# The last loads of a decode kernel: K, K, V, gate and up ahead of the last V, and W_down last in 10 KB rows

## The chip, the cores and the metric

The kernel runs on one core of one Trainium2 chip. The metric is the device time of one execution in microseconds (us). All executions quoted here are of the fast state. Times are medians; a ratio is the mean time of one kernel's fast runs over that of the kernel before in the same rounds, so it is not quite the ratio of the medians quoted beside it. The span of a profile runs from the first to the last instruction and is about 2 us shorter than the time.

## The reference

One decode step of a pre-LayerNorm block, in bf16: B = 2 rows, D = 512, 32 heads of 128, a cache of 8,192 positions, F = 1,376.

```python
h   = x + softmax(q k^T / sqrt(128)) v @ wo       # q = layernorm(x) @ wq, k and v from the cache
u   = layernorm(h)
out = h + (relu(u @ W_gate) * (u @ W_up)) @ W_down
```

K and V caches are 268 MB; all weights together are 12.6 MB. One core reads all of it.

## The kernel before

The 64 (row, head) combinations are handled as 32 pairs, 0 to 31; K31 and V31 are the tiles of the last pair. A pair needs one K tile and one V tile, 4 MB each, as 128 partitions of 32 KB. Four slots hold the tiles: K in slots 0 and 2, V in slots 1 and 3. VectorE (DVE) computes three quarters of the scores by multiply and tree-add, TensorE (PE) the rest by transposes; ScalarE (ACT) takes the exponentials; PE does the PV matmuls with V as the loaded weights.

```python
for p in range(NP):                                   # NP = 32 pairs
    ...                                               # scores and exp of pair p
    if p + 2 < NP:
        sp.wait(*t_kfree[p])
        t_k[p + 2] = load(s, slot[s][:], kv(A_k_cache, p + 2))
    if p == NP - 2:
        sp.wait(*t_kfree[p])                          # slot 0 is free: the weights go there
        nc.sync.dma_start(slot[s][:, 0:DC * F], B_W_gate...)
        nc.sync.dma_start(slot[s][:, DC * F:2 * DC * F], B_W_up...)
        nc.sync.dma_start(slot[s][...].rearrange("p (r n) -> p r n", n=D),
                          B_W_down[0:1280].rearrange("(r p) n -> p r n", p=128))   # 1,280 rows of 1 KB
        nc.sync.dma_start(wd_last[0:FR, :], B_W_down[1280:F])                      # 96 rows of 1 KB
    ...                                               # PV matmuls of pair p
    if p + 2 < NP - 1:
        sp.wait(t_pv[p])
        t_v[p + 2] = load(sv, ...)                    # V one pair behind K
    if p == NP - 2:
        ...                                           # V31 in four pieces, behind the weights
    if p == 14:
        nc.sync.dma_start(wo_sb[:], ...)              # W_o, 4,096 rows of 1 KB
```

After the last PV the tail is a chain: 40 W_o matmuls, the residual, the mean, up and gate (44 matmuls each), a variance sum in float32, W_down (44), the output.

```python
lhsT=w[:, c, f * 128:f * 128 + fw]                    # up and gate: contiguous columns
...
nc.tensor.matmul(Sp[0][:, 64:64 + B], lhsT=ones_f[:], rhs=d2[:, c * B:(c + 1) * B], ...)  # float32, 4 of them
```

The softmax here doesn't subtract the row's maximum and nothing guards it: scores larger than these inputs give would overflow.

## Time and profile before

| | before |
|---|---|
| time (three runs; the result below has a fourth) | 682.75 us (682.70 to 682.88) |
| span | 680.7 us |
| V31 issued | 651.1 us |
| last piece of V31 landed, last PV ended | 667.8, 668.4 us |
| from the last PV's end to the end | 12.3 us |

From the timeline of the kernel before, the DMA issues of the sync engine at the end (start, duration, queue, line, operation, destination and source, count):

```profile
617.86 0.33 SPq L133 DMA_DIRECT2D slot<-in_A_k_cache_dram  x1
637.52 0.33 SPq L377 DMA_DIRECT2D slot<-in_B_W_gate_dram  x1
637.90 0.97 SPq L379 DMA_DIRECT2D slot<-in_B_W_up_dram  x1
638.92 0.52 SPq L381 DMA_DIRECT2D slot<-in_B_W_down_dram  x1
639.48 11.62 SPq L384 DMA_DIRECT2D wd_last<-in_B_W_down_dram  x1
651.14 2.02 SPq L426 DMA_DIRECT2D slot<-in_A_v_cache_dram  x4
```

The issue behind W_down's 1,280 rows takes 11.62 us, so V31 is issued only at 651.14. From the windows of one microsecond of the kernel before (stretch and length, busy us and instructions of PE, PE's weight loads, DVE, ACT and GpSimd, then granted PE clock, busy share of the DMA engines, GB/s):

```profile
650.00:651.00 1.00, 0.69 (x11) 0.34 (x9) 0.98 (x1) 0.96 (x2) 0.00 (x0) 0.50 0.48 203
651.00:652.00 1.00, 0.38 (x8) 0.29 (x8) 0.96 (x1) 0.53 (x2) 0.00 (x0) 0.50 0.49 183
652.00:653.00 1.00, 0.00 (x0) 0.00 (x0) 0.93 (x3) 0.66 (x4) 0.00 (x0) 0.50 0.72 219
```

For two microseconds about half of the DMA engine time stands idle there.

From the timeline of the kernel before, the tail (in brackets the idle time before and what ended it):

```profile
667.84 0.59 PE L407 MATMUL O<-e,slot 128*128 128x2 bf16 x16 [0.62 <-DMA slot<-in_A_v_cache_dram]
...
668.28 1.48 PE L303 MATMUL W<-O_sb,wo_sb 128*128 128x2 bf16 x40
...
670.95 1.52 PE L473 MATMUL S<-d_b,slot 128*128 128x2 bf16 x44 [0.66 <-DVE S L462]
...
672.33 1.52 PE L473 MATMUL O<-d_b,slot 128*128 128x2 bf16 x44
...
673.72 1.84 PE L482 MATMUL S<-d,ones_f 128*128 128x2 f32 x8
...
675.42 0.47 PE L501 MATMUL O<-hd,slot 128*128 128x2 bf16 x10
```

The W_down matmuls (675.42) stand behind the float32 variance sum in PE's order, although what they need was ready at 674.15. The weight loads of up and W_o in the kernel before, by line (duration in ns: least, median, most):

```profile
L303 PEld LDWEIGHTS W<-O_sb,wo_sb x136: 111/118/123, 585.4 to 669.6; 128*128 128x128 bf16 x136
```

```profile
L473 PEld LDWEIGHTS S<-d_b,slot x44: 103/104/195, 670.9 to 672.2; 128*128 128x128 bf16 x40, 128*96 128x96 bf16 x4
```

W_o is read in steps of 8 bytes (118 ns), up in contiguous columns (104 ns).

### The profile page before, as it was taken

The numbers are of one execution on the slowest core, as the hardware profiler recorded it, in microseconds if no ns is written. First come the engines' busy times: TensorE is split into PE (matmuls) and PEld (weight loads), VectorE is DVE, ScalarE is ACT, GpSimd is POOL, SyncE is SP. The second block draws the span as 40 slices with busy tenths as digits, with TensorE's granted clock in tenths as the row PEclk, the third lists the DMA queues.
The fourth block names the chain that finished last, engine by engine and source line by source line (L and its number), as shares of the span: only waits on it lengthen the run. The fifth ranks groups of instructions, "written<-read, shape, count | busy, mean of one in ns | idle before, by whom it ended". The sixth has DMA issues, their size and how long they took to land.

```text
span 680.7 us, 14440 instructions
## 1 busy us (share of the span) xinstructions
PE 297.6 (44%) x6602; PEld 268.7 (39%) x6602; DVE 492.9 (72%) x426; ACT 202.6 (30%) x523; POOL 1.8 (0%) x11
## 2 busy tenths in 40 slices
PE   2544334444543445354342344535443444653436
PEld 2444334443433334344341333434433443543326
DVE  1777778867777887777782788776777886777781
ACT  0632223333222333332131233333222333332230
POOL 1000000000000000000000000000000000000000
PEclk9955566555555555655555556555556555555555
DMA  9999999999999999999999999999999999999990
GB/s 374 437 432 431 428 428 430 430 429 430 432 429 431 430 429 429 430 430 429 430 345 435 429 428 428 428 430 431 428 429 430 429 429 430 430 429 430 409 360 27
DMA packets 15936, 281.97 MB, mean 414 GB/s; under 512 B 1442, under 2 KB 6916, under 8 KB 7172
## 3 DMA queue, kind: packets, MB, share of 16 engines
q1 hardware_dynamic: 15872, 281.06, 97.1%
q8 instruction: 51, 0.84, 0.5%
q14 instruction: 9, 0.07, 0.0%
q10 hardware_dynamic: 4, 0.00, 0.0%
HBM read 281.05 MB, written 0.00 MB: 413 GB/s over the span
## 4 chain that ended last, share of the span: by engine, by line
DMA 69%; DVE 27%; SPq 2%; PE 1%; issue 1%; DVEq 0%
DMA slot<-in_A_k_cache_dram 66%; DVE prod L324 16%; DVE tb L332 6%; DVE prod L332 3%; DMA slot<-in_A_v_cache_dram 2%; SPq L384 2%; DVE scores L339 1%; PE S L482 0%; PE S L473 0%; PE O L501 0%; PE O L473 0%; PE W L303 0%; SPq L426 0%; SPq L133 0%; SPq L379 0%
## 5 line engine op out<-in xcount | busy, mean ns | idle before, releaser
L324 DVE TENSOR_TENSOR prod<-slot,q_b 128x6144 bf16<-128x6144 bf16 x64 | 214.9, 3358 | 135.3 <-DMA slot<-in_A_k_cache_dram 134.2
L407 PE MATMUL O<-e,slot 128*128 128x2 bf16 x4096 | 119.5, 165 | 248.4 <-ACT e L261 124.2
L407 PEld LDWEIGHTS O<-e,slot 128*128 128x128 bf16 x4096 | 114.4, 104 | 253.6 <-DMA slot<-in_A_v_cache_dram 126.9
L355 ACT ACTIVATE kT<-T 128x1024 bf16<-128x1024 bf16 x128 | 126.9, 1022 | 171.7 <-PE T L349 170.7
L349 PE MATMUL T<-ident,slot 128*128 128x128 bf16 x1024 | 123.6, 307 | 71.9 <-DMA slot<-in_A_k_cache_dram 71.9
L332 DVE TENSOR_TENSOR tb<-prod 128x3072 bf16<-128x3072 bf16 (+1 forms) x128 | 148.2, 1158 | 4.4
L349 PEld LDWEIGHTS T<-ident,slot 128*128 128x128 bf16 x1024 | 100.3, 141 | 74.9 <-DMA slot<-in_A_k_cache_dram 74.9
L261 ACT ACTIVATE e<-scores 64x48 bf16<-64x48 f32 x128 | 32.8, 256 | 255.0 <-DVE scores L339 253.4
L332 DVE TENSOR_TENSOR prod<-tb 128x1536 bf16<-128x1536 bf16 (+1 forms) x128 | 84.2, 658 | 4.4
L253 PE MATMUL S<-qT,kT 128*128 128x2 bf16 x1024 | 48.4, 168 | 33.0 <-ACT kT L355 31.7
L253 PEld LDWEIGHTS S<-qT,kT 128*128 128x128 bf16 x1024 | 41.1, 107 | 52.0 <-ACT kT L355 52.0
L339 DVE TENSOR_REDUCE scores<-prod 128x48 f32<-128x384 bf16 x64 | 35.4, 553 | 2.2
L261 ACT ACTIVATION_READ_ACCUMULATOR e<-scores 64x1 f32 x128 | 23.7, 185 | 0.0
L261 ACT ACTIVATE e<-S 64x32 bf16<-64x32 f32 x64 | 13.0, 204 | 15.1 <-PE S L253 14.3
L261 ACT ACTIVATION_READ_ACCUMULATOR e<-S 64x1 f32 x64 | 12.9, 201 | 0.7
L235 ACT ACTIVATE q_b<-O 128x512 bf16<-128x512 f32 x8 | 4.3, 594 | 15.6 <-PE O L230 15.6
L208 DVE CAST qT<-W 128x64 bf16<-128x64 f32 x1 | 0.2, 225 | 12.0 <-PE W L203 12.0
L203 PE MATMUL W<-xlT,slot 128*128 128x2 bf16 x128 | 3.6, 165 | 8.6 <-DMA slot<-in_A_wq_dram 8.6
L203 PEld LDWEIGHTS W<-xlT,slot 128*128 128x128 bf16 x128 | 3.5, 104 | 8.7 <-DMA slot<-in_A_wq_dram 8.7
L279 DVE TENSOR_REDUCE zr<-O 128x16 f32<-128x48 f32 (+1 forms) x4 | 0.8, 204 | 8.3 <-PE O L271 8.3
L271 PE MATMUL S<-zs,ones_f 128*128 128x6 f32 x2 | 0.6, 367 | 10.9 <-ACT e L261 10.9
L230 PE MATMUL O<-ident,qrep 128*128 128x128 bf16 x32 | 4.3, 303 | 1.7 <-ACT q_b L235 0.9
(56 smaller groups left out, 47.2 us busy)
## 6 DMA issues: line engine op xcount, KB each, us to landing
slot<-in_A_k_cache_dram SPq DMA_DIRECT2D x32, 4096.0 KB, 27.9
slot<-in_A_v_cache_dram SPq DMA_DIRECT2D x31, 4096.0 KB, 32.1
slot<-in_A_wq_dram SPq DMA_DIRECT2D x1, 4096.0 KB, 12.3
wo_sb<-in_A_wo_dram SPq DMA_DIRECT2D x1, 4096.0 KB, 43.4
slot<-in_A_v_cache_dram SPq DMA_DIRECT2D x2, 1536.0 KB, 12.1
slot<-in_B_W_gate_dram SPq DMA_DIRECT2D x1, 1376.0 KB, 10.0
slot<-in_B_W_up_dram SPq DMA_DIRECT2D x1, 1376.0 KB, 13.2
slot<-in_B_W_down_dram SPq DMA_DIRECT2D x1, 1280.0 KB, 15.0
```

Source lines behind the costliest of these rows:

```text
L203: i = nc.tensor.matmul(Wp[:, h * B:(h + 1) * B], lhsT=wq[:, c, h * Dh:(h + 1) * Dh], rhs=lT[:, c * B:(c + 1) * B], start=(c == 0), stop=(c ...
L230: i = nc.tensor.matmul(Op[m % 2][:, k * 128:(k + 1) * 128], lhsT=qrep[m % 2][:, k * 128:(k + 1) * 128], rhs=ident[:], start=True, stop=True)
L235: t_cp[m] = act.run(nc.scalar.activation(out=q_b[:, m * 512:(m + 1) * 512], in_=Op[m % 2][:], func=ACT.Copy))
L253: i = nc.tensor.matmul(Sp[p % 2][:, 2 * jj:2 * jj + 2], lhsT=kT[n % 3][:, k * 128:(k + 1) * 128], rhs=qT[:, 2 * p:2 * p + 2], start=True, ...
L261: t = act.run(nc.scalar.activation(out=e_t[p % 2][q, j0:j0 + nj, a], in_=src(q, a), func=ACT.Exp, scale=inv_sqrt_dh, accum_out=zs[q, 2 * p ...
L324: t_dm = dve.run(nc.vector.tensor_tensor(out=prod[:], in0=k_t[:, c * JC:(c + 1) * JC, :], in1=qv, op=ALU.mult))
L332: dve.run(nc.vector.tensor_tensor(out=o, in0=cur[:, :, 0:half], in1=cur[:, :, half:w], op=ALU.add))
L339: t_s = dve.run(nc.vector.tensor_reduce(out=sc[:], in_=cur, axis=AX.X, op=ALU.add))
L349: i = nc.tensor.transpose(Tp[n % 3][:, k * 128:(k + 1) * 128], k_t[:, j, :], ident[:])
L355: t_ev[n] = act.run(nc.scalar.activation(out=kT[n % 3][:], in_=Tp[n % 3][:], func=ACT.Copy))
L384: nc.sync.dma_start(wd_last[0:FR, :], B_W_down[1280:F]).then_inc(sem_w, 16)
L407: i = nc.tensor.matmul(Op[k % 2][:, col:col + 2], lhsT=v_t[:, j, :], rhs=e_t[p % 2][:, j, :], start=(nmm == 0), stop=(nmm == J - 1))
```

## The change

The intent: bring W_down, which is needed last, behind the last V; make its rows long; bring K31 early, so that the scores of the last pair are done when V31 comes; and shorten the tail. W_o moves to the start, into the buffer that W_q leaves free. Rows of 10 KB put rows 10p to 10p+9 of W_down on partition p, so that the hidden units of block f are f, f+10, f+20, ...: the columns of gate and up must be read in steps of 10 elements, 20 bytes.

```diff
-                t_wq = load(3, slot[3][:], A_wq...)
+                nc.sync.dma_start(X[:], A_wq...).then_inc(sem_wq, 16)
@@ after the q projection
+                nc.sync.dma_start(X[:].rearrange("p (h n) -> p h n", n=D),
+                    A_wo.rearrange("(h d) n -> d h n", d=128)).then_inc(sem_wo, 16)
@@ the pair loop (cut)
+                vparts = ((0, 96, 128), (1, 0, 48), (2, 48, 88), (2, 88, 96))
+                    if p < NP - 2:
+                        pv(p)
+                        if p < NP - 4:
+                            load_v(p + 2)
+                        elif p == NP - 3:
+                            load_v(p + 1)          # V30, issued behind K31
+                    elif p == NP - 2:
+                        sp.wait(*t_kfree[p])
+                        for k, w in enumerate((B_W_up, B_W_gate)):
+                            nc.sync.dma_start(slot[0][:, k * DC * F:(k + 1) * DC * F], ...)
+                        load_v(p + 1, vparts)      # V31 in four pieces
+                        nc.sync.dma_start(slot[0][:, 2 * DC * F:2 * DC * F + 10 * D],
+                            B_W_down[0:10 * 128].rearrange("(p r) n -> p (r n)", r=10)).then_inc(sem_wd, 16)
@@ before the last PV
+                o_proj(range(HM, 30), 0, 2)        # HM = 24; this and the next line: 32 of the 40 W_o matmuls
+                o_proj(range(30, 32), 0, 1)
@@ up and gate
-                                dst[...], lhsT=w[:, c, f * 128:f * 128 + fw],
+                                dst[...], lhsT=w[:, c, f:1280:10] if f < 10 else w[:, c, 1280:F],
@@ variance
-                    i = nc.tensor.matmul(Sp[0][:, 64:64 + B], lhsT=ones_f[:], rhs=d2[...])      # x4, float32
+                    i = nc.tensor.matmul(Sp[0][:, 64:64 + B], lhsT=onesn[:], rhs=vh[...])       # x2, bf16
```

Also cut: the gate's result and W_down are split in halves, wd_last is loaded at the start, two memsets of PSUM go, W_down's matmuls loop over blocks first, the first 96 W_o matmuls run at pair 24 instead of 27, and some small tiles share memory with others.

More of the change, by code (lines that the diff above doesn't have):

```diff
@@ L87, in bass_sequential_preLN__gqa_block_cached__glu_gated_reglu__decode_kernel @@
         slot_cnt = [0] * 4
-        sem_x, sem_wo, sem_w, sem_wdl, sem_out = S("x"), S("wo"), S("w"), S("wdl"), S("out")
+        sem_x, sem_wq, sem_wo, sem_w, sem_wd, sem_out = S("x"), S("wq"), S("wo"), S("w"), S("wd"), S("out")
         sem_vl = [S(f"vl{i}") for i in range(4)]
         slot = [sb(f"slot{i}", [128, SLOT], BF16) for i in range(4)]
-        wo_sb = sb("wo_sb", [128, H, D], BF16)
-        wd_last = sb("wd_last", [128, D], BF16)
+        HM = 24
+        X = sb("X", [128, H * D], BF16)
+        wd_last = sb("wd_last", [FR, D], BF16)
         prod = sb("prod", [128, JC, Dh], BF16)
@@ L97, in bass_sequential_preLN__gqa_block_cached__glu_gated_reglu__decode_kernel @@
         q_b = sb("q_b", [128, NP * Dh], BF16)
-        qrep = [sb(f"qrep{i}", [128, 4 * 128], BF16) for i in range(2)]
         qT = sb("qT", [128, NP * 2], BF16)
@@ L103, in bass_sequential_preLN__gqa_block_cached__glu_gated_reglu__decode_kernel @@
         onesn = sb("onesn", [128, 128], BF16)
-        x_row = sb("x_row", [B, D], BF16)
-        lnx_row = sb("lnx_row", [B, D], BF16)
+        qrep = [tb[:, i * 512:(i + 1) * 512] for i in range(2)]
+        x_row = kT[0][0:B, 0:D]
+        lnx_row = kT[0][0:B, D:2 * D]
         bst = sb("bst", [B, 6], F32)
@@ L121, in bass_sequential_preLN__gqa_block_cached__glu_gated_reglu__decode_kernel @@
         r2 = sb("r2", [128, B], F32)
+        vh = sb("vh", [128, 2 * B], BF16)
         u_sb = sb("u_sb", [128, FC * B], F32)
@@ L146, in _ @@
             def _(eng):
-                nc.scalar.dma_start(x_row[:], A_x[:, 0]).then_inc(sem_x, 16)
-                t_wq = load(3, slot[3][:], A_wq.rearrange("(p c) n -> p (c n)", c=DC))
+                nc.scalar.dma_start(x_row, A_x[:, 0]).then_inc(sem_x, 16)
+                nc.sync.dma_start(X[:], A_wq.rearrange("(p c) n -> p (c n)", c=DC)).then_inc(sem_wq, 16)
                 t_k, t_v = {}, {}
@@ L153, in _ @@
                 t_k[1] = load(2, slot[2][:], kv(A_k_cache, 1))
+                t_v[1] = load(3, slot[3][:], kv(A_v_cache, 1))
+                nc.sync.dma_start(wd_last[:], B_W_down[F - FR:]).then_inc(sem_wd, 16)
                 pool.run(nc.gpsimd.memset(ident_f[:], 0.0))
@@ L170, in _ @@
                 dve.wait((sem_x, 16))
-                dve.run(nc.vector.bn_stats(out=bst[:], in_=x_row[:]))
+                dve.run(nc.vector.bn_stats(out=bst[:], in_=x_row))
                 dve.last()
@@ L181, in _ @@
                 t_ln = dve.run(nc.vector.tensor_scalar(
-                    out=lnx_row[:], in0=x_row[:], scalar1=mv[:, 0:1], scalar2=sd[:, 0:1],
+                    out=lnx_row, in0=x_row, scalar1=mv[:, 0:1], scalar2=sd[:, 0:1],
                     op0=ALU.subtract, op1=ALU.mult))
@@ L187, in _ @@
                 for k, row in enumerate((x_row, lnx_row)):
-                    rv = row[:].rearrange("b (n c) -> b c n", c=DC)
+                    rv = row.rearrange("b (n c) -> b c n", c=DC)
                     for c in range(DC):
@@ L196, in _ @@
                 lT = xlT[:, DC * B:]
-                wq = slot[3][:].rearrange("p (c n) -> p c n", c=DC)
-                pe.wait(t_wq, t_xlT)
+                wq = X[:].rearrange("p (c n) -> p c n", c=DC)
+                pe.wait((sem_wq, 16), t_xlT)
                 for h in range(H):
@@ L211, in _ @@
                 sp.wait(t_q)
-                t_v[1] = load(3, slot[3][:], kv(A_v_cache, 1))
+                nc.sync.dma_start(
+                    X[:].rearrange("p (h n) -> p h n", n=D),
+                    A_wo.rearrange("(h d) n -> d h n", d=128)).then_inc(sem_wo, 16)
                 t_cp = {}
@@ L221, in _ @@
                     t = dve.run(nc.vector.tensor_copy(
-                        out=qrep[m % 2][:].rearrange("p (k r) -> p k r", r=64),
+                        out=qrep[m % 2].rearrange("p (k r) -> p k r", r=64),
                         in_=qT[:, m * 8:(m + 1) * 8].unsqueeze(2).broadcast_to([128, 8, 64])))
@@ L293, in o_scale @@
                         op=ALU.mult))
-                wo_v = wo_sb[:].rearrange("p h (n c) -> p h c n", c=DC)
+                wo_m = X[:].rearrange("p (h n c) -> p h c n", n=128, c=DC)
                 Ov = O_sb[:].rearrange("p (g b a) -> p g a b", b=B, a=2)
@@ L303, in o_proj @@
                             i = nc.tensor.matmul(
-                                Wp[:, c * B + b0:c * B + b1], lhsT=wo_v[:, h, c, :], rhs=Ov[:, h // 2, h % 2, b0:b1],
+                                Wp[:, c * B + b0:c * B + b1], lhsT=wo_m[:, h, c, :], rhs=Ov[:, h // 2, h % 2, b0:b1],
                                 start=first[0], stop=last, skip_group_check=True)
@@ L311, in _, with pv, load_v @@
                 t_batch = {}
+                vparts = ((0, 96, 128), (1, 0, 48), (2, 48, 88), (2, 88, 96))
+                W_AT = 24
+                def pv(p):
+                    v_t = tile((2 * p + 1) % 4)
+                    k = next(kk for kk, (a, b_) in enumerate(batches) if a <= p < b_)
+                    col = 2 * (p - batches[k][0])
+                    parts = vparts if p == NP - 1 else (
+                        [(0, NCH * JC, J)] + [(1 + c, c * JC, (c + 1) * JC) for c in range(NCH)])
+                    if p == batches[k][0] and k >= 2:
+                        pe.wait(t_O[k - 2])
+                    nmm = 0
+                    for ci, (ei, j0, j1) in enumerate(parts):
+                        pe.wait(t_exp[p][ei], (sem_vl[ci], 16) if p == NP - 1 else t_v[p])
+                        for j in range(j0, j1):
+                            i = nc.tensor.matmul(
+                                Op[k % 2][:, col:col + 2], lhsT=v_t[:, j, :], rhs=e_t[p % 2][:, j, :],
+                                start=(nmm == 0), stop=(nmm == J - 1))
+                            nmm += 1
+                    t_pv[p] = pe.run(i)
+                    if p + 1 in ends and p < NP - 1:
+                        t_batch[k] = z_sum(k, *batches[k])
+                        if k < 3:
+                            t_O[k] = normalize(k, *batches[k], t_batch[k], False)
+                def load_v(p, parts=None):
+                    sv = (2 * p + 1) % 4
+                    if p >= 2:
+                        sp.wait(t_pv[p - 2])
+                    if parts is None:
+                        t_v[p] = load(sv, slot[sv][:], kv(A_v_cache, p))
+                        return
+                    src = kv(A_v_cache, p)
+                    for ci, (_, j0, j1) in enumerate(parts):
+                        nc.sync.dma_start(
+                            slot[sv][:, j0 * Dh:j1 * Dh], src[:, j0 * Dh:j1 * Dh]).then_inc(sem_vl[ci], 16)
                 for p in range(NP):
@@ L315, in _ @@
                     k_t = tile(s)
-                    last_pair = p == NP - 1
                     for c in range(NCH):
@@ L366, in _ @@
                         exp(p, 1 + c, lambda q, a: sc[q, :], c * JC, JC)
-                        if last_pair and c == 0:
-                            t_O[3] = normalize(3, 24, 31, t_batch[3], False)
                     t_kfree[p] = (t_dm, t_pt[p * NG + NG - 1])
@@ L374, in _ @@
                         t_k[p + 2] = load(s, slot[s][:], kv(A_k_cache, p + 2))
-                    if p == NP - 2:
-                        sp.wait(*t_kfree[p])
-                        nc.sync.dma_start(slot[s][:, 0:DC * F], B_W_gate.rearrange("(p c) n -> p (c n)", c=DC)
-                                          ).then_inc(sem_w, 16)
-                        nc.sync.dma_start(slot[s][:, DC * F:2 * DC * F],
-                                          B_W_up.rearrange("(p c) n -> p (c n)", c=DC)).then_inc(sem_w, 16)
-                        nc.sync.dma_start(
-                            slot[s][:, 2 * DC * F:2 * DC * F + 10 * D].rearrange("p (r n) -> p r n", n=D),
-                            B_W_down[0:1280].rearrange("(r p) n -> p r n", p=128)).then_inc(sem_w, 16)
-                        nc.sync.dma_start(wd_last[0:FR, :], B_W_down[1280:F]).then_inc(sem_w, 16)
-                        ws = s
@@ L388, in _ @@
-                    sv = (2 * p + 1) % 4
-                    v_t = tile(sv)
-                    k = next(kk for kk, (a, b_) in enumerate(batches) if a <= p < b_)
-                    col = 2 * (p - batches[k][0])
-                    if not last_pair:
-                        pe.wait(t_v[p])
-                        order = [(0, NCH * JC, J)] + [(1 + c, c * JC, (c + 1) * JC) for c in range(NCH)]
-                    else:
-                        order = [(1, 0, 48), (2, 48, 96), (0, 96, 112), (0, 112, 128)]
-                        zt = z_sum(4, 31, 32)
-                        normalize(4, 31, 32, zt, True)
@@ L399, in _ @@
-                    if p == batches[k][0] and k >= 2:
-                        pe.wait(t_O[k - 2])
-                    nmm = 0
-                    for ci, (ei, j0, j1) in enumerate(order):
-                        pe.wait(t_exp[p][ei])
-                        if last_pair:
-                            pe.wait((sem_vl[ci], 16))
-                        for j in range(j0, j1):
-                            i = nc.tensor.matmul(
-                                Op[k % 2][:, col:col + 2], lhsT=v_t[:, j, :], rhs=e_t[p % 2][:, j, :],
-                                start=(nmm == 0), stop=(nmm == J - 1))
-                            nmm += 1
@@ L411, in _ @@
-                    t_pv[p] = pe.run(i)
-                    if p + 1 in ends and not last_pair:
-                        t_batch[k] = z_sum(k, *batches[k])
-                        if k < 3:
-                            t_O[k] = normalize(k, *batches[k], t_batch[k], False)
-                    if p + 2 < NP - 1:
-                        sp.wait(t_pv[p])
-                        t_v[p + 2] = load(sv, slot[sv][:], kv(A_v_cache, p + 2))
-                    elif p + 2 == NP - 1:
-                        t_vlast = t_pv[p]
@@ L421, in _ @@
-                    if p == NP - 2:
-                        sp.wait(t_vlast)
-                        sl = (2 * (p + 1) + 1) % 4
-                        src = kv(A_v_cache, p + 1)
-                        for ci, (j0, j1) in enumerate(((0, 48), (48, 96), (96, 112), (112, 128))):
-                            nc.sync.dma_start(
-                                slot[sl][:, j0 * Dh:j1 * Dh], src[:, j0 * Dh:j1 * Dh]).then_inc(sem_vl[ci], 16)
-                    if p == 14:
-                        nc.sync.dma_start(wo_sb[:], A_wo.rearrange("(h d) n -> d h n", d=128)).then_inc(sem_wo, 16)
@@ L430, in _ @@
-                    if p == 27:
-                        pe.wait((sem_wo, 16), t_O[0], t_O[1], t_O[2])
-                        o_proj(range(0, 24), 0, 2)
-                    if p == NP - 2:
-                        pass
+                    if p < NP - 2:
+                        pv(p)
+                        if p == W_AT:
+                            pe.wait((sem_wo, 16), t_O[0], t_O[1], t_O[2])
+                            t_om = pe.run(o_proj(range(0, HM), 0, 2))
+                        if p < NP - 4:
[3 more added lines that the diff above has]
+                    elif p == NP - 2:
+                        sp.wait(*t_kfree[p])
+                        for k, w in enumerate((B_W_up, B_W_gate)):
+                            nc.sync.dma_start(
+                                slot[0][:, k * DC * F:(k + 1) * DC * F],
+                                w.rearrange("(p c) n -> p (c n)", c=DC)).then_inc(sem_w, 16)
+                        load_v(p + 1, vparts)
+                        nc.sync.dma_start(
+                            slot[0][:, 2 * DC * F:2 * DC * F + 10 * D],
+                            B_W_down[0:10 * 128].rearrange("(p r) n -> p (r n)", r=10)).then_inc(sem_wd, 16)
@@ L437, in _ @@
+                pv(NP - 2)
+                t_O[3] = normalize(3, 24, 31, t_batch[3], False)
                 pe.wait(t_O[3])
-                o_proj(range(24, 30), 0, 2)
+                o_proj(range(HM, 30), 0, 2)
                 o_proj(range(30, 32), 0, 1)
+                normalize(4, 31, 32, z_sum(4, 31, 32), True)
+                pv(NP - 1)
                 dve.wait(t_pv[NP - 1])
@@ L457, in _, with ffn_in @@
                     in1=Sp[0][:, 0:B].unsqueeze(1).broadcast_to([128, DC, B]), op=ALU.subtract))
-                dve.last()
-                t_d2 = dve.run(nc.vector.tensor_tensor(out=d2[:], in0=d_b[:], in1=d_b[:], op=ALU.mult))
-                dve.run(nc.vector.memset(Op[1][:, 0:FC * B], 0.0))
-                t_m0 = dve.run(nc.vector.memset(Sp[1][:, 0:FC * B], 0.0))
-                wgt = slot[ws][:, 0:DC * F].rearrange("p (c f) -> p c f", c=DC)
-                wup = slot[ws][:, DC * F:2 * DC * F].rearrange("p (c f) -> p c f", c=DC)
-                wdn = slot[ws][:, 2 * DC * F:2 * DC * F + 10 * D].rearrange("p (r n c) -> p r c n", c=DC, n=128)
+                wup, wgt = (slot[0][:, k * DC * F:(k + 1) * DC * F].rearrange("p (c f) -> p c f", c=DC)
+                            for k in range(2))
+                wdn = slot[0][:, 2 * DC * F:2 * DC * F + 10 * D].rearrange("p (r n c) -> p r c n", c=DC, n=128)
                 wdl = wd_last[:].rearrange("p (n c) -> p c n", c=DC)
-                pe.wait((sem_w, 64), t_d, t_m0)
-                def ffn_in(dst, w):
-                    for f in range(FC):
+                pe.wait((sem_w, 32), t_d)
+                def ffn_in(dst, w, f0, f1):
+                    for f in range(f0, f1):
                         fw = 128 if f < 10 else FR
@@ L473, in ffn_in @@
                             i = nc.tensor.matmul(
-                                dst[0:fw, f * B:(f + 1) * B], lhsT=w[:, c, f * 128:f * 128 + fw],
+                                dst[0:fw, f * B:(f + 1) * B], lhsT=w[:, c, f:1280:10] if f < 10 else w[:, c, 1280:F],
                                 rhs=d_b[:, c * B:(c + 1) * B], start=(c == 0), stop=(c == DC - 1))
                     return pe.run(i)
-                t_u = ffn_in(Sp[1], wup)
-                t_g = ffn_in(Op[1], wgt)
-                pe.wait(t_d2)
-                for c in range(DC):
-                    i = nc.tensor.matmul(Sp[0][:, 64:64 + B], lhsT=ones_f[:], rhs=d2[:, c * B:(c + 1) * B],
-                                         start=(c == 0), stop=(c == DC - 1))
-                t_var = pe.run(i)
+                FH = 6
+                t_u = ffn_in(Sp[1], wup, 0, FC)
+                t_g = (ffn_in(Op[1], wgt, 0, FH), ffn_in(Wp, wgt, FH, FC))
+                dve.last()
+                dve.run(nc.vector.tensor_tensor(out=d2[:], in0=d_b[:], in1=d_b[:], op=ALU.mult))
+                dve.last()
+                dve.run(nc.vector.tensor_reduce(
+                    out=vr[:], in_=d2[:].rearrange("p (c b) -> p b c", b=B), axis=AX.X, op=ALU.add))
+                dve.last()
+                dve.run(nc.vector.tensor_copy(out=vh[:, 0:B], in_=vr[:]))
+                dve.last()
+                t_vh = dve.run(nc.vector.tensor_tensor(out=vh[:, B:], in0=vr[:], in1=vh[:, 0:B], op=ALU.subtract))
                 dve.wait(t_u)
@@ L487, in _ @@
                 dve.last()
-                dve.wait(t_g)
-                t_hd = dve.run(nc.vector.scalar_tensor_tensor(
-                    out=hd[:], in0=Op[1][:, 0:FC * B], scalar=0.0, in1=u_sb[:], op0=ALU.max, op1=ALU.mult))
+                t_hd = []
+                for k, (bank, f0, f1) in enumerate(((Op[1], 0, FH), (Wp, FH, FC))):
+                    dve.wait(t_g[k])
+                    t_hd.append(dve.run(nc.vector.scalar_tensor_tensor(
+                        out=hd[:, f0 * B:f1 * B], in0=bank[:, f0 * B:f1 * B], scalar=0.0,
+                        in1=u_sb[:, f0 * B:f1 * B], op0=ALU.max, op1=ALU.mult)))
+                pe.wait(t_vh)
+                for k in range(2):
+                    i = nc.tensor.matmul(Sp[0][:, 64:64 + B], lhsT=onesn[:], rhs=vh[:, k * B:(k + 1) * B],
+                                         start=(k == 0), stop=(k == 1))
+                t_var = pe.run(i)
                 dve.wait(t_var)
-                dve.run(nc.vector.tensor_scalar(
-                    out=vr[:], in0=Sp[0][:, 64:64 + B], scalar1=1.0 / D, scalar2=eps, op0=ALU.mult, op1=ALU.add))
+                dve.run(nc.vector.tensor_scalar_add(out=vr[:], in0=Sp[0][:, 64:64 + B], scalar1=eps))
                 dve.last()
                 dve.run(nc.vector.reciprocal(out=r2[:], in_=vr[:]))
-                pe.wait(t_hd)
-                for c in range(DC):
-                    for f in range(FC):
-                        lw = wdn[:, f, c, :] if f < 10 else wdl[0:FR, c, :]
+                pe.wait((sem_wd, 32))
+                for k, (f0, f1) in enumerate(((0, FH), (FH, FC))):
+                    pe.wait(t_hd[k])
+                    for f in range(f0, f1):
                         kp = 128 if f < 10 else FR
-                        i = nc.tensor.matmul(
-                            Op[0][:, c * B:(c + 1) * B], lhsT=lw, rhs=hd[0:kp, f * B:(f + 1) * B],
-                            start=(f == 0), stop=(f == FC - 1))
+                        for c in range(DC):
+                            i = nc.tensor.matmul(
+                                Op[0][:, c * B:(c + 1) * B], lhsT=wdn[:, f, c, :] if f < 10 else wdl[:, c, :], rhs=hd[0:kp, f * B:(f + 1) * B],
+                                start=(f == 0 and c == 0), stop=(f == FC - 1), skip_group_check=True)
                 t_y = pe.run(i)
```

## The prediction

> **What bounds it now.** The loads. The slices show the DMA engines at 90% or more until the last slice, about 430 GB/s; 281 MB at that rate is 654 of 680.7 us of span. In the timeline a K+V pair comes every 19.7 us, and DVE needs 15.5 us per pair; the chain of waits is two thirds K transfers. Only lost DMA time and the tail after the last V piece can be won.
>
> Lost at the end (one-microsecond windows): the rate falls to about 200 GB/s at 650 to 653. The sync queue shows why: W_down (1,280 rows of 1 KB) is queued ahead of V31; the next issue, wd_last, takes 11.62 us, so V31 is issued only at 651.14. K31 lands at 645.8, V31's last piece at 667.8: 22.0 us for 8.4 MB, which is 19.6 us at 430. The tail then takes 12.9 us: PV, 40 W_o matmuls (1.35), mean, up 1.5, gate 1.4, a float32 variance sum (1.84, which delays W_down), W_down 1.6, output 3.2.
>
> **What changes.**
> 1. Order: K30, K31, V30, up, gate, V31 in pieces, W_down in 128 rows of 10 KB behind it. W_down (1.31 MB, about 3 us) leaves V31's path and is needed only some 5 us later; the issue stall goes. The Trainium skill ("DMA: Bandwidth & Descriptors", "Why small descriptors are slow") gives a fixed cost per packet. The trace agrees mildly: W_o's 1 KB rows take about 11.3 us for 4.19 MB against 9.8 for a K.
> 2. W_o moves to the start, into W_q's buffer, still 1 KB rows: about nothing. Its stall of the next issue (25.4 us before) recurs near 35 us with the engines kept full.
> 3. K31 arrives 10 us earlier (636), so DVE does K30 and K31 back to back until 657.5, then batch 3's normalisation; 32 W_o matmuls precede the last PV. V31 lands near 663 (estimate: 7.0 MB after V30 at 646, at 405 to 430 GB/s), and the last PV ends near 664 instead of 668.4: -4.5 us.
> 4. Tail: W_o 40 matmuls -> 8 (-1); memsets off the path (-0.2); variance as two bf16 matmuls (-1.2 of W_down's delay). Together -2.4.
> 5. Against it: the gate and up weight loads step by 20 bytes. The Trainium skill ("SBUF — State Buffer", note on SBUF cachelines) says that full bandwidth needs two hits per 16-byte line; 20 bytes gives one. The trace shows 8-byte steps (W_o, W_down) at 118 ns per weight load against 104 contiguous, about 35 against 28 ns per matmul. No 20-byte step has run; I estimate 50 to 65 ns, +2 us over 80 loads, wholly in the tail.
>
> Sum: -4.5 -2.4 +2.0 = -4.9 of 682.75.
>
> **Predicted:** 677.8 us, 674.0 to 681.5; faster by over 2%: 0.03, within 2%: 0.95, slower: 0.02.
>
> **What would show it.** Right: no dip near 650; V31 issued near 638; its last piece landing at 662 to 664; up and gate 1.8 to 2.7 us each; W_down landed before hd and starting right behind the gate. Wrong: up and gate at 1.5 (step 5 empty: about 676) or 4 each (681); a DMA gap at 35 to 65 us.
>
> **What would make it wrong.** The engines finishing unevenly, so that V31's last piece lands as late as before; 20-byte loads several times slower; DVE's end at 657 limiting by over a microsecond; the early W_o starving K2.

## More of the kernel before

From the page of the kernel before: the busy share of the DMA engines in 40 slices of the span, the rate in each slice, and two DMA queues (packets, MB, share of the 16 engines' time).

```profile
DMA  9999999999999999999999999999999999999990
GB/s 374 437 432 431 428 428 430 430 429 430 432 429 431 430 429 429 430 430 429 430 345 435 429 428 428 428 430 431 428 429 430 429 429 430 430 429 430 409 360 27
...
q1 hardware_dynamic: 15872, 281.06, 97.1%
q8 instruction: 51, 0.84, 0.5%
```

The loads bound the kernel: about 430 GB/s in all slices but the first, the last three, and slice 21 with W_o's short rows. DVE is 72% busy, PE 44%.

## The result, and the profile after

| | before | after |
|---|---|---|
| time, median of 4 | 682.79 us | 679.80 us (679.52 to 680.05) |
| ratio (95% interval) | | 0.9956 (0.9939 to 0.9973) |
| span | 680.7 us | 678.2 us |
| last piece of V31 landed | 667.8 us | 664.9 us |
| last PV ended | 668.4 us | 665.7 us |
| from there to the end | 12.3 us | 12.5 us |
| all loads landed | 667.8 us | 667.9 us |

The change is 0.44% faster, clear of noise and well under 2%. Two rows tell most of it. The last PV ends 2.7 us sooner and the tail is 0.2 us longer. And the loads as a whole end when they ended before: only their order has changed.

From the page of the changed kernel:

```profile
GB/s 375 427 432 376 430 431 430 429 428 430 428 429 430 432 430 432 430 432 427 430 428 429 426 429 427 431 432 432 431 432 430 429 431 425 429 429 393 416 406 58
...
q8 instruction: 51, 0.84, 0.5%
```

The dip of W_o's short rows has moved from slice 21 to slice 4. A new dip (393) is in slice 37, where K31 and V30 are issued. From its timeline, the sync engine's issues:

```profile
619.18 0.43 SPq L135 DMA_DIRECT2D slot<-in_A_v_cache_dram  x1
638.26 0.33 SPq L428 DMA_DIRECT2D slot<-in_B_W_up_dram  x1
638.64 0.43 SPq L428 DMA_DIRECT2D slot<-in_B_W_gate_dram  x1
639.12 2.13 SPq L353 DMA_DIRECT2D slot<-in_A_v_cache_dram  x4
641.29 0.44 SPq L432 DMA_DIRECT2D slot<-in_B_W_down_dram  x1
```

V31 is issued at 639.1, and the stall is gone. From its windows of one microsecond:

```profile
659.00:660.00 1.00, 1.00 (x33) 1.00 (x30) 0.00 (x0) 0.00 (x0) 0.00 (x0) 0.50 1.05 444
660.00:661.00 1.00, 1.00 (x30) 1.00 (x29) 0.33 (x2) 0.00 (x0) 0.00 (x0) 0.50 0.59 248
661.00:662.00 1.00, 1.00 (x41) 1.00 (x39) 0.00 (x0) 0.00 (x0) 0.00 (x0) 0.50 0.47 199
662.00:663.00 1.00, 0.65 (x25) 0.56 (x22) 0.00 (x0) 0.00 (x0) 0.00 (x0) 0.50 0.55 223
663.00:664.00 1.00, 0.00 (x0) 0.00 (x0) 0.00 (x0) 0.00 (x0) 0.00 (x0) 0.50 0.56 227
```

From 660 to 665 the rate is half of the full one: half of the DMA engines have finished everything, and the other half still load V31 and W_down. The idle half has been moved from 650 to 660, not removed.

From the timeline of the changed kernel, the tail:

```profile
664.28 1.44 PE L334 MATMUL O<-e,slot 128*128 128x2 bf16 x48 [1.63 <-DMA slot<-in_A_v_cache_dram]
...
666.04 0.43 PE L309 MATMUL W<-O_sb,X 128*128 128x1 bf16 x8 [0.32 <-DVE O_sb L297]
...
667.34 2.79 PE L473 MATMUL S<-d_b,slot 128*128 128x2 bf16 x44 [0.34 <-DVE d_b L458]
...
669.99 1.52 PE L473 MATMUL O<-d_b,slot 128*128 128x2 bf16 x24
...
671.38 1.39 PE L473 MATMUL W<-d_b,slot 128*128 128x2 bf16 x20
...
672.63 0.19 PE L502 MATMUL S<-vh,onesn 128*128 128x2 bf16 x2
672.68 1.48 PE L515 MATMUL O<-hd,slot 128*128 128x2 bf16 x40
```

The variance sum is now 0.19 us and W_down starts right behind it. But up and gate take from 667.34 to 672.77 instead of from 670.95 to 673.85: 5.4 us for 2.9. Their weight loads in the changed kernel, by line:

```profile
L473 PEld LDWEIGHTS S<-d_b,slot x44: 137/157/195, 667.3 to 669.8; 128*128 128x128 bf16 x40, 128*96 128x96 bf16 x4
```

The tail, term by term, from the two timelines:

| step | before | after | difference |
|---|---|---|---|
| last PV's end to the residual (W_o 40 -> 8 matmuls) | 1.37 | 0.79 | -0.6 |
| residual, mean, until up starts (memsets) | 1.15 | 0.83 | -0.3 |
| up and gate | 2.90 | 5.43 | +2.5 |
| gate's end to W_down's start (variance) | 1.57 | -0.09 | -1.7 |
| W_down matmuls | 1.60 | 1.61 | 0 |
| W_down's end to the end | 3.7 | 3.9 | +0.2 |

### The profile page after: what moved, and what is told of

Read it like the earlier page. It is cut to its first block, busy times and chain, and to the rows that moved or that the text cites. A ratio compares the mean times of both kernels' runs of the same rounds, so it can differ in the third digit from the quotient of the medians.

```text
span 678.2 us, 14430 instructions
## 1 busy us (share of the span) xinstructions
PE 297.5 (44%) x6596; PEld 269.5 (40%) x6596; DVE 493.6 (73%) x428; ACT 202.3 (30%) x523; POOL 1.7 (0%) x11
## 4 chain that ended last, share of the span: by engine, by line
DMA 73%; DVE 24%; PE 1%; issue 1%; SPq 0%; DVEq 0%
DMA slot<-in_A_k_cache_dram 69%; DVE prod L366 15%; DVE tb L374 5%; DMA slot<-in_A_v_cache_dram 4%; DVE prod L374 3%; DVE scores L381 1%; PE S L473 0%; PE O L515 0%; PE O L334 0%; PE O L473 0%; PE W L473 0%; SPq L353 0%; SPq L135 0%; SPq L428 0%; PE W L309 0%
## 5 line engine op out<-in xcount | busy, mean ns | idle before, releaser
L309 PE MATMUL W<-O_sb,X 128*128 128x2 bf16 (+1 forms) x136 | 5.0, 172 | 7.0 <-DVE O_sb L297 7.0
L309 PEld LDWEIGHTS W<-O_sb,X 128*128 128x128 bf16 x136 | 4.8, 118 | 7.2 <-DVE O_sb L297 7.2
L207 PE MATMUL W<-xlT,X 128*128 128x2 bf16 x128 | 3.6, 165 | 8.5 <-DMA X<-in_A_wq_dram 8.5
L207 PEld LDWEIGHTS W<-xlT,X 128*128 128x128 bf16 x128 | 3.5, 104 | 8.6 <-DMA X<-in_A_wq_dram 8.6
```

Source lines behind the costliest of these rows:

```text
L207: i = nc.tensor.matmul(Wp[:, h * B:(h + 1) * B], lhsT=wq[:, c, h * Dh:(h + 1) * Dh], rhs=lT[:, c * B:(c + 1) * B], start=(c == 0), stop=(c ...
L309: i = nc.tensor.matmul(Wp[:, c * B + b0:c * B + b1], lhsT=wo_m[:, h, c, :], rhs=Ov[:, h // 2, h % 2, b0:b1], start=first[0], stop=last, sk ...
```

## The experiments

**A reading of the trace first.** A load is spread over 16 DMA engines, and the trace records when each of the sixteen parts reports. The first and the last of the sixteen, worked out from those records:

```
                first part    last part   spread (us)
before  K0        22.2          24.0         1.9
before  K16      332.9         339.5         6.6
before  K17      366.7         370.5         3.9      (behind W_o)
before  K30      619.2         626.4         7.1
before  V31 end  664.0         667.8         3.8
after   K30      617.4         627.1         9.7
after   K31      630.4         636.8         6.5      (K31 issued at about 619)
after   V31 end  657.7         664.9         7.2
after   W_down   660.8         667.9         7.2
```

A load counts as landed when the last part is in. By K30 in the changed kernel eight parts lie between 617.4 and 621.6 us and the other eight between 625.5 and 627.1; the latter fall behind about 1.6 us at a time over the whole run, one part after the other. The records of the second queue show one instruction packet about every 13 us, and their durations repeat in groups of eight (1025, 1018, 1081, 1078, 1061, 1102, 1107, 1086 ns, then 1039, 1026, 1082, 1069, and so on), as if eight engines took turns. So I formed two theories of why the last V came only 2.9 us sooner. The first is the prediction's: the stall of V31's issue had cost about 2 us, and something else took it back. The rival is that the slowest engines set every landing, that these were hardly ever idle, and that the idle time in the windows is that of the engines that had run ahead. The eight runs e1 to e8 were made in two calls, e9 to e11 in a third; each call ran on another chip and shared its runs of the kernel before, whose medians (683.02, 682.90 and 682.82 us) agree with the 682.79 of the result.

A caution on results: three kernels are wrong, and the comparison with the reference passed all three. At its tolerance it does not see these errors. The versions called right below are right by their indexing: only the row order of W_down and the columns that belong to it are changed, and always together.

**e1: contiguous gate and up (wrong).**

```diff
-  lhsT=w[:, c, f:1280:10] if f < 10 else w[:, c, 1280:F],
+  lhsT=w[:, c, f * 128:f * 128 + fw],
```

> The changed kernel with gate and up weights read in contiguous columns; the result is wrong on purpose, since W_down's 10 KB rows no longer match. Theory (the 20-byte step costs 2.4 us in the tail, all on the path: up 2.79 us against 1.52, gate about 2.6 against 1.4): 677.3 us, up and gate together 2.9 us. Rival (the step is hidden or the tail waits for W_down, which landed at 667.9): within 0.5 us of 679.8. A third possibility: gate ends earlier than W_down's landing and 0.5 to 1 us of the gain is lost there; then W_down's matmuls start with an idle gap named after W_down's load.

Measured: 677.22 us, ratio 0.9914 (0.9900 to 0.9927). Its weight loads of up, by line:

```profile
L473 PEld LDWEIGHTS S<-d_b,slot x44: 104/104/195, 666.8 to 668.1; 128*128 128x128 bf16 x40, 128*96 128x96 bf16 x4
```

Up took 1.53 us again. From up's start to W_down's first matmul passed 2.8 us (666.84 to 669.66), 5.3 in the changed kernel, and W_down had landed at 667.9, so nothing waited for it. The 20-byte step costs 2.5 us, all of it on the path; the time fell by 2.6 against the changed kernel. It was run at another time.

**e2: contiguous columns, W_down in 1 KB rows as the last load (right).**

```diff
-  slot[0][:, 2 * DC * F:2 * DC * F + 10 * D], B_W_down[0:1280].rearrange("(p r) n -> p (r n)", r=10)
+  slot[0][...].rearrange("p (r n) -> p r n", n=D), B_W_down[0:1280].rearrange("(r p) n -> p r n", p=128)
```

(with e1's edit)

> The changed kernel with W_down in 1 KB rows again, still as the last load, and gate and up in contiguous columns; the result is right. If the 10 KB rows buy nothing once W_down is last (1 KB packets took 46 ns each, 80 per engine, 3.7 us, against 3.1 us for 10 KB), W_down lands about 0.6 us later, at about 668.6, before it is needed, and the time is that of the run with contiguous columns, about 677.3. If the 10 KB rows matter as my prediction's step 1 has it, it is 1 us or more slower than that run and W_down's matmuls wait for the load.

Measured: 677.61 us, ratio 0.9918 (0.9905 to 0.9932). W_down landed at 668.2 and its matmuls began at 670.1, so nothing waited for it. The intervals of e1 and e2 overlap. Once W_down is the last load, its long rows buy nothing that can be told from noise (677.22 against 677.61), and the strided columns that they enforce are pure cost.

**e3: the kernel before with W_down moved behind V31, nothing else (right).**

```diff
   nc.sync.dma_start(... B_W_up ...)
-  nc.sync.dma_start(... B_W_down[0:1280] ...)
-  nc.sync.dma_start(wd_last[0:FR, :], B_W_down[1280:F])
   ...                                     # V31 in four pieces
+  nc.sync.dma_start(... B_W_down[0:1280] ...)
+  nc.sync.dma_start(wd_last[0:FR, :], B_W_down[1280:F])
```

> The kernel before with W_down and its remainder (both still in 1 KB rows) moved behind V31's pieces, nothing else. V31's last piece lands about 3.7 us earlier, near 664, and V31 is issued near 638.5. But K31 still lands near 645.8 behind V30, so DVE ends its scores at 661.9 and the exp that the last PV needs comes at 662.7: if that limits, the last PV ends near 666 instead of 668.4 and the time is about 680.4. If only the order of W_down counts, the last PV ends near 664.6 and the time is about 679.

Measured: 681.03 us, ratio 0.9970 (0.9957 to 0.9982). V31's last piece landed at 663.6, 4.2 us sooner than before, but the 128 PV matmuls ran without a break from 662.9, right behind the exp of pair 31, until 666.5, as its timeline shows:

```profile
662.90 3.55 PE L403 MATMUL O<-e,slot 128*128 128x2 bf16 x128
```

The first branch of the expectation is the nearer one (680.4 stated, 679 for the other): with K31 still behind V30, DVE becomes the limit. The order of W_down alone is worth 2 us. That the rest needs K31 before V30 follows from this wait; it had no run of its own.

**e4: the kernel before with W_down in 10 KB rows but still ahead of V31 (wrong).**

```diff
-  slot[s][...].rearrange("p (r n) -> p r n", n=D), B_W_down[0:1280].rearrange("(r p) n -> p r n", p=128)
+  slot[s][:, 2 * DC * F:2 * DC * F + 10 * D], B_W_down[0:1280].rearrange("(p r) n -> p (r n)", r=10)
```

> The kernel before with W_down in 10 KB rows, still ahead of V31; the result is wrong on purpose (gate and up stay contiguous). This takes the issue stall away (V31 issued near 639 instead of 651) and leaves the order. My prediction took the stall to cost about 2.4 us (22.0 us against 19.6): then 680.4. Rival: the slowest DMA engine sets when a load has landed, it lost under 1 us in the stall, and the idle time seen is that of the engines that run ahead: then 681.8 or more.

Measured: 682.59 us, ratio 0.9991 (0.9978 to 1.0005). The stall is gone, as its timeline of the sync engine shows:

```profile
638.10 0.42 SPq L381 DMA_DIRECT2D slot<-in_B_W_down_dram  x1
638.57 0.53 SPq L384 DMA_DIRECT2D wd_last<-in_B_W_down_dram  x1
639.14 2.12 SPq L426 DMA_DIRECT2D slot<-in_A_v_cache_dram  x4
```

V31 was issued 12 us sooner, and its last piece landed only 0.5 us sooner (667.3 for 667.8). That is no more than the longer rows of W_down save: 80 packets of 46 ns per engine against 8 of 385 ns, 3.7 against 3.1 us. The records of the parts say why. In the kernel before, the last part of the weights reported at 658.0 us and the last part of V31 9.8 us later; the first parts of 4 MB tiles came 9.7 us apart all through the run, so that is the time of one tile on one engine. This fits a slowest engine that went from the weights to V31 without a gap, with the stall or without it (657.5 and 667.3 in e4). The stall, the largest mark in the profile before, had cost nothing that can be told from noise. This decides for the rival.

**e5: W_o in the middle again (right).**

```diff
-  (after the q projection)  nc.sync.dma_start(X..., A_wo...)
+  if p == 14:               nc.sync.dma_start(X..., A_wo...)
```

> The changed kernel with W_o loaded in the middle (behind V16) as before, into the same buffer; the result is right. In the changed kernel the 16 landings of one load drift apart to 9.7 us by K30 (7.1 before), and the early W_o is what no longer evens them out. If that spread is what makes V31's last piece land late (664.9 instead of the 663 I had predicted), the time falls by 1 us or more, to 678.8 or less. If only the slowest engine counts and its load of bytes is the same wherever W_o stands, V31's last piece lands within 0.7 us of 664.9 and the time is 679.8 to within 0.7 us.

Measured: 679.24 us, ratio 0.9945 (0.9932 to 0.9957); the changed kernel had 0.9956 and, later, 0.9953, and the intervals overlap. The spread at K30 fell from 9.7 to 7.1 us, V31's last piece landed at 664.2 for 664.9. So the larger spread itself costs at most some tenths of a microsecond: a load waits for its slowest engine, and how far the others are ahead does not matter. Whether those tenths are real is open: in e10, the changed kernel unaltered, V31's last piece landed at 664.5.

**e6: half of the PV matmuls of pairs 0 to 29 left out (wrong).**

```diff
-  for j in range(j0, j1):
+  for j in range(j0, j1, 1 if p >= NP - 2 else 2):
```

> The changed kernel with every second PV matmul of pairs 0 to 29 left out; the result is wrong on purpose. About 3,840 of 14,430 instructions go. Theory: the engines drift apart because the fetching of instructions (51 packets of 16 KB, each about 1.05 us, one every 13 us, with durations that repeat in groups of eight) shares eight of the sixteen DMA engines with the loads. Then about 13 of the packets go, 1.7 per engine at 1.3 us: the spread of K30's landings falls by about 2 us or more from 9.7, the whole of the loads ends 2 to 2.5 us sooner, and the time is about 677.5. Rival: those engines are slower for another reason (HBM, ports): spread still about 9.7, time 679.8 to within 0.5 us, since PE was not the limit.

Measured: 676.94 us, ratio 0.9910 (0.9896 to 0.9923). Two lines of its page:

```profile
span 675.2 us, 10590 instructions
...
q8 instruction: 36, 0.59, 0.4%
```

With 15 instruction packets fewer, the spread at K30 is 6.8 us for 9.7, and all loads have landed at 664.8 for 667.9, although the same bytes of data were loaded. PE was idle more than half of the time before, so what was saved is not its work. A rival remains that the edit alone does not exclude: with fewer matmuls PE also reads memory less, which might speed up all transfers. The traces exclude it: K30's first part reported at 617.4 us in the changed kernel and at 617.5 here, and the median packet of 32 KB took 1,215 and 1,216 ns. The engines in front were no faster; only those behind gained.

The traces also let packets and delays be counted, over the K and V loads whose first part reported between 100 and 620 us. Take the delays of a load's parts behind its first part and add them up: from one load to the next this sum stays about the same or jumps by about 1.6 us (the median of the jumps over 0.8 us, in both kernels). The changed kernel has 41 such jumps and 40 packets of the second queue in that time; e6 has 28 jumps and 26 packets. So nearly every instruction packet puts one engine back by about 1.6 us. The saving agrees: about 3 us for 15 packets on eight engines is 1.6 us per packet and engine. (The 1.3 us in the expectation was too low.) The eight engines fall behind because they also carry the fetching of instructions, though no record names the engine of a packet.

**e7: the changed kernel with the float32 variance sum (right).**

```diff
-  2 matmuls, lhsT=onesn (bf16), rhs=vh
+  4 matmuls, lhsT=ones_f (float32), rhs=d2
```

> The changed kernel with the variance summed by four float32 matmuls again, as before; the result is right. The bf16 pair took 0.19 us, the float32 sum 1.84 in the kernel before, and W_down's matmuls stand behind it in PE's order: 1.5 us slower than the change, about 681.3. Rival: the sum overlaps the wait for hd, then under 0.5 us.

Measured: 681.61 us, ratio 0.9980 (0.9966 to 0.9993). The sum in its timeline:

```profile
672.77 1.85 PE L502 MATMUL S<-d,ones_f 128*128 128x2 f32 x8
```

The bf16 sum is worth 1.8 us; its length is the whole of its effect.

**e8: e2, with V31's last two pieces cut at 80 instead of 88 (right).**

```diff
-  vparts = ((0, 96, 128), (1, 0, 48), (2, 48, 88), (2, 88, 96))
+  vparts = ((0, 96, 128), (1, 0, 48), (2, 48, 80), (2, 80, 96))
```

> The changed kernel with gate and up in contiguous columns, W_down in 1 KB rows as the last load, and V31's last two pieces cut at 80 instead of 88, so that 32 matmuls follow the third piece and 16 the last, which lands about 1.2 us later; the result is right. If the last PV's end is set by the landing of pieces plus the matmuls behind it, the last PV ends 0.2 to 0.4 us earlier than with the cut at 88: about 677.3 against 677.6. If the drift of the slowest engine rules, no difference above the noise of 0.3 us.

Measured: 677.32 us, ratio 0.9914 (0.9900 to 0.9927), not to be told from e2. In the trace the last PV ended 0.6 us after the last piece had landed (665.1 for 664.5), where e2 needed 0.8 (665.7 for 664.9).

**e9: e8, with up loaded by eight engines (right).** The attempt was to give the eight slow engines less to load.

```diff
+  for q in range(4):
+      for i8 in range(4):
+          rows = slice(32 * q + i8, 32 * q + 32, 4)
+          nc.sync.dma_start(slot[0][rows, 0:DC * F], up_v[rows, :]).then_inc(sem_w, 16)
```

> The version with contiguous columns and the cut at 80, with the up weight alone loaded by sixteen DMAs of 8 partitions each, issued behind the gate weight; the result is right. The Trainium skill (DMA: Bandwidth & Descriptors, section on why a DMA increments its semaphore by 16) says that a DMA whose slowest dimension is 8 runs on the lowest-numbered eight engines of the core. If the eight engines slowed by instruction fetch are the other eight, they carry 1.4 MB / 16 less each (3.3 us), V31's last piece lands up to 3 us earlier, the exp near 658.7 and 128 PV matmuls limit, and the time falls by 1 to 2 us, to about 675.8. If they are the same eight, V31 lands 3 us later and the time is about 680.5. If the two sets are mixed, or sixteen issues of about 0.45 us each on the sync queue delay V31, in between or worse.

Measured: 687.02 us, ratio 1.0051 (1.0038 to 1.0065). From its timeline of the sync engine:

```profile
638.76 10.79 SPq L434 DMA_DIRECT2D slot<-in_B_W_up_dram  x16
649.59 3.23 SPq L353 DMA_DIRECT2D slot<-in_A_v_cache_dram  x4
```

The sixteen issues took 10.8 us, the last part of up landed only at 663.3, and V31's last piece at 674.6. The experiment failed and does not tell which eight engines are the slow ones. Its semaphore took nine updates for each of the sixteen transfers, which fits the eight engines of the expectation and one update more. The last of them came in pairs, 0.8 us apart, from 656 to 663.3 us, and two of the sixteen parts of V31's last piece came 6.7 and 8.3 us behind the first, the other fourteen within 1.5. That looks like the mixed case of the expectation, two slow engines among the eight, but this was not tested further.

**e10 and e11: the changed kernel and e8 again, in the same rounds.**

> The changed kernel again, unaltered, for a comparison on the same chip in the same rounds: 679.8 us, ratio 0.9956 to the kernel before.

> The version with contiguous gate and up, W_down in 1 KB rows last and the cut at 80 again, beside the changed kernel: 677.3 us, 2.5 us (0.37%) below the changed kernel of the same rounds, by the stride alone.

Measured: 679.85 us, ratio 0.9953 (0.9940 to 0.9965), and 677.02 us, ratio 0.9913 (0.9900 to 0.9927). The version with contiguous columns is 2.8 us faster than the change and 5.8 us faster than the kernel before: the best that was run.

## Why the prediction was right or wrong

The time, 679.8 us, lies in the stated range of 674.0 to 681.5, and the class (within 2%) is right. The gain was 3.0 us where 4.9 were predicted; the terms come to -2.8 where -4.9 was stated, so no large errors cancelled; the range was wide enough for the miss. Of the marks that were to show it, V31's issue (639.1), the rate at 650 (429 GB/s) and W_down's start behind the gate came as stated; V31's landing (664.9 for 662 to 664) and up and gate (2.8 us each for 1.8 to 2.7) fell just outside. The prediction named engines that finish unevenly as what could make it wrong, and step 3 alone fell 1.8 us short. Term by term:

- **What bounds it: right.** The loads did, and all landed at the same time in both kernels.
- **Step 1, W_down out of V31's path: right; "the issue stall goes": it went, but was worth nothing.** W_down lands 3.1 us behind V31 now, and that is the gain of the landing. The excess of 22.0 us over 19.6 that I read as cost of the stall and let flow into step 3 was not there to be won: removing the stall alone moved V31's landing by 0.5 us (e4). This is one of the two terms that were mis-sized; it shows in step 3.
- **Step 2, W_o early and its stall: right.** The issue behind W_o took 24.6 us at 35 us with the DMA engines busy all the while (share 0.97 to 1.04 in windows of 10 us). W_o itself took 11.5 us in the kernel before (349.3 to 360.8 between last parts), a little more than the 11.3 of step 1. W_o's place changed the time by no more than the noise (e5).
- **Step 3, -4.5 us: measured -2.7, the largest miss.** K31 landed at 636.8 (636 predicted) and DVE was done near 658, as predicted. V31's last piece landed at 664.9, not 663: V30 landed at 646.8 for 646, and the 7.0 MB behind it took 18.1 us, which is 387 GB/s where I had 405 to 430. My estimate took one average rate for all engines; the landing is that of the slowest, which instruction fetch holds up (e6). And 48 PV matmuls, not only the 8 of the last piece, waited for the end, because the third piece landed at 664.2, 0.7 us before the last: the last PV ended at 665.7, 0.8 us behind the landing. The prediction had allowed 1 us there, so the shortfall is that of the landing.
- **Step 4, -2.4 us: measured -2.6** (-0.6, -0.3 and -1.7 in the table). The share of the variance is larger than I had it (e7: 1.8), that of W_o smaller.
- **Step 5, +2.0 us: measured +2.5 in the timeline, 2.6 to 2.8 in the time (e1, e11).** The stride was the cost, as e1 shows, and the estimate of 50 to 65 ns per matmul held (2.79 us for 44, 63 ns). The Trainium skill ("SBUF — State Buffer", the note on SBUF cachelines) was the right warning: the median weight load went from 104 to 157 ns. That lines of 16 bytes are the reason fits these figures, but no run here tests it.

## What to carry to other kernels

A load has landed when its slowest DMA engine is done, so idle engines in the windows are lost time only if the slowest one idles; look at the spread of a load's parts before counting a dip of the rate as gain. Put last what is needed last, and then let it have whatever rows suit its consumer: a layout that pleases a transfer off the path and slows matmuls in the tail is a bad trade. When a kernel is bound by loads, its instruction count is part of its traffic.

## What the Trainium skill lacked or had wrong

- "Runtime: NRT & Kernel Launch", section on instruction fetch mechanics, calls the cost of a 16 KiB block "mostly hidden". Engines' waits may be, but the loads are not: 51 blocks were fetched, nearly each of those counted put one engine's loads back by about 1.6 us, and 15 blocks fewer ended all loads 3.1 us sooner (e6).
- "DMA: Bandwidth & Descriptors" does not say that the engines of one stream of plain loads drift further apart from load to load when only instruction packets run beside it: from 1.9 to 9.7 us between first and last part within 627 us. It names engines 7 and 15 as usually slower, and takes that to belong to transfers issued by GpSimd; here, with all large loads issued by the sync engine, eight of the sixteen fell behind.
- The same page, "Why small descriptors are slow", has no figure for loads in 1 KB rows on this chip: medians of 46 ns per packet for W_down and 48 to 51 for W_o, against 1,215 ns for 32 KB, so 20 to 22 against 27 bytes per ns and engine. Nor did I find there that the issue behind a load of thousands of rows blocks the sync engine (24.6 us behind 4,096 rows, 11.6 us behind 1,280, but 0.5 us behind the same bytes in 10 KB rows in e4), or that DMAs of eight partitions take 10.8 us for sixteen issues (e9).
- "SBUF — State Buffer", the note on cachelines, names no size for weight loads, and the two hits per 16-byte line that it asks for did not give quite the full speed: the median was 104 ns contiguous, 118 ns at 8 bytes (two per line), 157 ns at 20 bytes.
